# An FFT filter ahead of a Gelu layer: table loads and table builds of the first batch put in another order

## Chip, cores, metric

The kernel runs on one core of one Trainium2 chip. The metric is the device time of one execution in microseconds (us). Each kernel is run several times; a single run scatters by some tenths of a us, and some runs by 1.5 to 3.8 us (told below), so parts of a us are read from traces, and times only confirm the sum.

## The reference

```python
X = np.fft.rfft(x, axis=1)                    # x: 8 batches, 3008 tokens, 256 channels
y = np.fft.irfft(X * (filt_r + 1j * filt_i)[None], n=3008, axis=1)
h = y.reshape(24064, 256) @ w_in              # 256 -> 2048
g = 0.5 * h * (1.0 + erf(h / sqrt(2)))        # exact Gelu
out = g @ w_out                               # 2048 -> 256
```

## The kernel before

The transform of 3008 = 47 x 64 points is done with matmuls in four stages. TensorE writes each result into a PSUM bank, and an *eviction* (`_evac`) copies it out, so that the bank can be used again; VectorE (DVE), ScalarE (ACT) and GpSimd (POOL) do the rest. Batch 0 has its own fast path (stages `c1` to `c4`, with transposes `c1t` and `c3t` between them), the *prelude*, in which nothing else can run. Then comes the *loop*: 47 tiles of 512 tokens, 16 slots each, with the two layers (`mm1` and Gelu, `mm2`) on TensorE in every slot; the transforms of the later batches (`s1` to `s4`) are put into chosen slots. The second layer starts at slot 16.

Sine and Gelu are functions of ACT. The trace has two table loads on ACT, one at the start (0.74 us) and one ahead of the first Gelu (29.66 us), each of 1.28 us; the second is brought on by a dummy Gelu on one column.

```python
def table_2_sin(self, h):                     # half h of the second table
    self.nc.scalar.activation(out=self.T2[:, 12 * h:12 * h + 12, 1, :], in_=self.gen[:, h], func=AF.Sin, scale=2.0 * PI)

def table_3(self, q, eng):                    # 8 transposes, one eviction of 128x1024
    ps = self.bank("ps_t3", "n", BF16)
    for i in range(8):
        self.nc.tensor.transpose(ps[:, 128 * i:128 * i + 128], self.T2[:, 8 * q + i, 1:3]..., self.eye)
    self._evac(self.T3[:, 8 * q:8 * q + 8], ps..., eng)

def c2(self, p):                              # 4 matmuls of 256, then the product on VectorE
    ps = self.bank("ps_c2", "w")              # two buffers
    ...
    nc.vector.tensor_tensor(out=w, in0=ps, in1=f..., op=ALU.mult)   # f: filter rows, partly copied by GpSimd

# ---- prelude (cut) ----
m.dup_filters(nc.gpsimd, 4, 4); m.load_w_in(); m.dup_filters(nc.gpsimd, 8, 8)
for u in range(16):                           # first stage
    m.c1(u // 2, u % 2, act if u < 4 or u % 2 else False)
    ...
m.table_2_sin(1)
m.c1t(0, False); m.c1t(1, act)
for q in range(7):
    if q < 6:
        m.c2(2 * q)
        if q > 0 and q + 2 < 6: m.c1t(q + 2, act)
        m.c2(2 * q + 1)
    if q == 0: m.table_3(0, act); m.table_2_swap(1); ...; m.c1t(2, act)
    if 1 <= q < 3: m.table_3(q, act)
    if q >= 1:
        if q < 6: m.c3(2 * q - 2)
        else: m.table_4(); m.c3(10, 1); m.c3(11, 1)      # table_4 makes T4 and T4c
    if q == 4: nc.scalar.activation(out=warm, in_=m.p, func=AF.Gelu)
```

Products are counted from 0 in the code (`c2(4)` makes the fifth). The pool "n" of `c1t`, `c3` and the tables has four PSUM banks.

Of the kernel before, what the change touches and what calls it, by code (L numbers as in the profile page):

```python
# [9 lines left out]
AF = mybir.ActivationFunctionType  # L10
ALU = mybir.AluOpType
FP32 = mybir.dt.float32
BF16 = mybir.dt.bfloat16
# [4 lines left out]
NA, NB = 47, 64  # L18
K1 = 24
# [9 lines left out]
class _Mix:  # L29
# [187 lines left out]
        ts(out=self.wtc, in0=self.p, scalar1=4.0, scalar2=1.0, op0=ALU.is_ge, op1=ALU.add)  # L217


    def table_4(self):  # L220
        nc = self.nc
        ps = self.bank("ps_t4", "n")
        rows = ((self.T4, self.T1p, self.wt), (self.T4c, self.T1q, self.wtc))
        o = [ps[0:96, 128 * i:128 * i + 2 * NA] for i in range(2)]
        for i, (t4, t1, wt) in enumerate(rows):
            nc.tensor.matmul(o[i], lhsT=t1.rearrange("p a b c -> p (a b c)"),
                             rhs=self.eye[0:2 * NA, 0:2 * NA], start=True, stop=True)
        for i, (t4, t1, wt) in enumerate(rows):
            self._evac(t4.rearrange("p n h -> p h n"), o[i].rearrange("p (h n) -> p h n", h=2), "act", wt[0:96])

    def table_3(self, q, eng):
        ps = self.bank("ps_t3", "n", BF16)
# [277 lines left out]
@with_exitstack  # L510
def kernel(
    ctx: ExitStack,
    tc: tile.TileContext,
    x: bass.AP,
    filt_r: bass.AP,
    filt_i: bass.AP,
    moe_w_in: bass.AP,
    moe_w_out: bass.AP,
    out: bass.AP,
):  # L520
    m = _Mix(ctx, tc, x, filt_r, filt_i, moe_w_in, moe_w_out, out)
    nc, B, S = tc.nc, m.B, m.S
    NT = B * S // TCH
    ctx.enter_context(tc.manual_schedule())

    g = m.small
    wide = ctx.enter_context(ExitStack())
    m.psum(wide, w=(2, 2), n=(4, 1))
    act = "act"
    m.p = m.iota(g, "p", [128, 1], [[0, 1]], cm=1)  # L530
    m.load_x(0, 0, 1, (0,))
    m.pi = m.iota(g, "pi", [128, 1], [[0, 1]], cm=1, dt=I32)
    m.load_x(0, 0, 1, (1,))
    m.ones = g.tile([128, 512], BF16, name="ones")
    nc.vector.memset(m.ones, 1.0)
    m.warm_up(10)
    m.table_1(g)
    m.weights_4(g)
    m.T1c = g.tile([2 * NA, 96], BF16, name="T1c")
    nc.vector.tensor_copy(out=m.T1c.rearrange("p (k h r) -> p k h r", h=2, r=2),  # L540
                          in_=m.T1.rearrange("p (h r k) -> p k h r", h=2, r=2))
    m.kk = m.iota(g, "kk", [128, K1 // 2], [[1, K1 // 2]])
    m.jj = g.tile([128, NB], FP32, name="jj")
    for sgn, lo in ((1, 0), (-1, 32)):
        nc.gpsimd.iota(m.jj[:, lo:lo + 32], pattern=[[sgn * NA, 32]], base=min(0, sgn * NA),
                       channel_multiplier=0, allow_small_or_imprecise_dtypes=True)
    cols = m.iota(g, "cols", [128, 128], [[1, 128]])
    m.load_x(0, 1, 4)
    m.gen = m.py.tile([128, 3, K1 // 2, NB], FP32, tag="y", name="gen")
    m.table_2(g)  # L550
    m.table_2_angle(0)
    m.unit_matrices(g, cols)
    m.table_2_angle(1)
    for k, n in ((0, 4), (4, 4), (8, 8), (16, 8)):
        m.load_filters(k, n)
    m.dup_filters(nc.gpsimd, 4, 4)
    m.load_w_in()
    m.dup_filters(nc.gpsimd, 8, 8)


    warm = g.tile([128, 1], FP32, name="warm")
    for u in range(16):
        m.c1(u // 2, u % 2, act if u < 4 or u % 2 else False)
        if u == 3:
            m.warm_up(3)
            m.table_2_sin(0)
        if u == 7:
            m.table_2_swap(0)
            m.table_2_minus()
            m.warm_up(3)  # L570
        if u == 11:
            m.warm_up(2)
    m.table_2_sin(1)
    m.warm_up(2)
    m.c1t(0, False)
    m.c1t(1, act)
    m.dup_filters(nc.vector, 0, 4)
    for q in range(7):
        if q < 6:
            m.c2(2 * q)  # L580
            if q > 0 and q + 2 < 6:
                m.c1t(q + 2, act)
            m.c2(2 * q + 1)
        if q == 0:
            m.table_3(0, act)
            m.table_2_swap(1)
            m.dup_filters(nc.gpsimd, 16, 8)
            m.T1p = g.tile([2 * NA, 2, K1, 2], BF16, name="T1p")
            nc.gpsimd.tensor_copy(out=m.T1p, in_=m.T1.rearrange("p (h r k) -> p h k r", h=2, r=2))
            m.T1q = g.tile([2 * NA, K1, 2, 2], BF16, name="T1q")  # L590
            nc.gpsimd.tensor_copy(out=m.T1q, in_=m.T1.rearrange("p (h r k) -> p k r h", h=2, r=2))
            m.table_1_tiles(g)
            m.load_x(1)
            m.load_w_out(0)
            m.load_w_out(8)
            m.c1t(2, act)
        if 1 <= q < 3:
            m.table_3(q, act)
        if q >= 1:
            if q < 6:  # L600
                m.c3(2 * q - 2)
            else:
                m.table_4()
                m.c3(10, 1)
                m.c3(11, 1)
        if q == 4:

            nc.scalar.activation(out=warm, in_=m.p, func=AF.Gelu)
    wide.close()
    wide = ctx.enter_context(ExitStack())  # L610
    m.psum(wide, v=(5, 1), t=(3, 1))
    for u in range(10):
        if u < 8:
            m.c3t(u)
        if u >= 2:
            m.c4(u - 2, (act, False if u > 7 else act))
    wide.close()
    m.psum(ctx, h=(3, 1), o=(2, 1), f=(3, 1))


    at = {}

    def put(slot, f, *a):
        at.setdefault(slot, []).append((f, a))

    def first(b):
        return (b * S // TCH) * 16

    for b in range(1, B):
        hi = first(b)  # L630
        if b == 1:
            s1, n1, r1, s2, n2, r2, s4, n4 = 0, 4, 15, 25, 2.8, 61, 68, 0.72
        else:
            s1, n1, r1, s2, n2, r2, s4, n4 = hi - 94, 3.5, hi - 80, hi - 69, 3.5, hi - 24, hi - 17, 1
        for u in range(16):
            put(s4 + int(u * n4), m.s4, b, u // 2, u % 2)
        for c in range(4):
            put(s1 + int(c * n1), m.s1, b, c)
            put(r1, m.r1, b, c)
            put(r2, m.r2, b, c)  # L640
        for p in range(12):
            put(s2 + int(n2 * p), m.s2, b, p)
            put(s2 + int(n2 * p) + 4, m.s3, b, p)
        if b + 1 < B:
            for i in range(8):
                put(s2 + int(n2 * (i + 2)), m.load_next, b, i + 2, i // 2, i % 2)

    for s in range((NT + 1) * 16):
        t, jc = s // 16, s % 16
        for f, a in at.pop(s, ()):  # L650
            f(*a)
        if t >= 1:
            m.mm2(t - 1, jc)
        if t < NT:
            m.mm1(t, jc)
    assert not at
# [30 lines left out]
```

## Time and profile before

| what | before |
|---|---|
| median of four runs (lowest, highest) | 774.23 us (774.01, 775.79) |
| span of the profiled run; granted clock of TensorE, as a share of full speed | 772.4 us; 1.000 |
| first `c1t` matmul (end of the first stage) | 14.22 us |
| VectorE's products | 16.40 to 31.84 us |
| transposes `c3t` start | 33.55 us |
| y of batch 0 complete | 40.96 us |
| first second-layer matmul (slot 16) | 51.31 us |

The page's busy times say little here: TensorE is busy everywhere. The page of before:

```profile
PE 757.2 (98%) x5965; PEld 528.4 (68%) x6066; DVE 397.8 (52%) x722; ACT 567.0 (73%) x980; POOL 64.8 (8%) x161
```

What matters is that the profile names no wait of TensorE after slot 16, and that the 51 us ahead of it are a relay between four engines. The moments of the table are read from the engines' timelines (start of the row, or start plus length).

### The profile page before, as it was taken

To read this page: it belongs to the slowest core of one execution; us is meant where nothing else is said; L and a number is where in the kernel's file an instruction comes from. 1 tells how busy PE (TensorE), PEld (TensorE's weight loads), DVE (VectorE), ACT (ScalarE), POOL (GpSimd) and SP (SyncE) were. 2 spreads that over 40 slices of the span, in tenths; PEclk is the share of its full clock that TensorE was granted. 3 is DMA by queue.
4 is the path that set the end of the run, shared out by engine and by line. 5 is a ranking of instruction groups with operands and counts; after the bars stand their busy time and mean duration, and the time that the engine had idled before them with its cause. 6 is when DMAs were issued, how large, how long until landed. Compare 5 with 4: busy or idle time off the path is not lost.

```text
span 772.4 us, 14959 instructions
## 1 busy us (share of the span) xinstructions
PE 757.2 (98%) x5965; PEld 528.4 (68%) x6066; DVE 397.8 (52%) x722; ACT 567.0 (73%) x980; POOL 64.8 (8%) x161
## 2 busy tenths in 40 slices
PE   7899999999999999999999999999999999999998
PEld 4857775676776766677777776666776676766666
DVE  8866755464555645456463664637646366411011
ACT  6879955897568975699656996579865798666663
POOL 8801100020000200011000110001100000000000
PEclk9999999999999999999999999999999999999999
DMA  9895645456153661636516364254543422410111
GB/s 144 138 179 133 146 119 129 128 121 155 56 139 108 138 152 46 191 81 123 143 52 182 85 133 123 78 155 97 122 137 80 139 83 69 123 42 28 42 42 55
DMA packets 87398, 85.66 MB, mean 111 GB/s; under 512 B 6752, under 2 KB 77536, under 8 KB 87328
## 3 DMA queue, kind: packets, MB, share of 16 engines
q1 hardware_dynamic: 78816, 68.70, 31.2%
q0 software_dynamic: 8512, 16.00, 14.1%
q8 instruction: 47, 0.77, 0.4%
q14 instruction: 23, 0.19, 0.1%
HBM read 54.00 MB, written 46.66 MB: 130 GB/s over the span
## 4 chain that ended last, share of the span: by engine, by line
PE 96%; ACT 1%; DVE 1%; issue 1%; POOL 0%; DVEq 0%; POOLq 0%
PE ps_o L492 43%; PE ps_h L465 39%; PE ps_s L324 3%; PE ps_s L349 3%; PE ps_s L299 2%; PE ps_s L276 2%; PE ps_c L409 1%; PE ps_c L387 0%; PE ps_c3t L428 0%; ACT T L249 0%; PE ps_c L442 0%; ACT vt_sb L249 0%; PE ps_e L482 0%; PE ps_c1t L375 0%; ACT at_sb L249 0%
## 5 line engine op out<-in xcount | busy, mean ns | idle before, releaser
L468 ACT ACTIVATE g_sb<-ps_h 128x512 bf16<-128x512 f32 x752 | 437.9, 597 | 183.0 <-PE ps_h L465 154.6
L492 PE MATMUL ps_o<-w_out_sb,g_sb 128*128 128x256 bf16 x2992 | 447.5, 273 | 2.1
L465 PE MATMUL ps_h<-y_sb,w_in_sb 128*128 128x512 bf16 (+3 forms) x1500 | 424.2, 365 | 0.2 <-issue 0.2
L492 PEld LDWEIGHTS <-g_sb 128*128 128x128 bf16 x2992 | 283.9, 98 | 134.4 <-issue 9.9
L465 PEld LDWEIGHTS <-w_in_sb 128*128 128x128 bf16 x1600 | 154.8, 98 | 23.2 <-issue 1.2
L498 DVE COPY ost<-ps_o 128x512 f32<-128x512 f32 x93 | 63.9, 687 | 143.8 <-PE ps_o L492 143.7
L307 DVE TENSOR_TENSOR p<-ps_s,F 128x512 bf16<-128x512 f32 x84 | 58.1, 692 | 105.2 <-ACT p L306 89.1
L253 DVE TENSOR_SCALAR y_sb<-ps_s 128x376 bf16<-128x376 f32 x112 | 61.0, 548 | 80.5 <-PE ps_s L349 80.5
L251 DVE CAST a_sb<-ps_s 128x512 bf16<-128x512 f32 x112 | 69.5, 684 | 27.4 <-PE ps_s L276 27.1
L251 DVE CAST v_sb<-ps_s 128x512 bf16<-128x512 f32 x84 | 57.4, 685 | 2.9 <-PE ps_s L324 2.8
L305 ACT ACTIVATE p<-ps_s 64x512 bf16<-64x512 f32 x84 | 49.8, 593 | 2.0
L306 ACT CAST p<-ps_s 64x512 bf16<-64x512 f32 x84 | 48.5, 577 | 1.0
L349 PEld LDWEIGHTS <-d_sb 96*128 96x128 bf16 x448 | 30.8, 97 | 25.2
L101 POOL COPY gate<-p 1x1 bf16<-1x1 bf16 x48 | 8.5, 176 | 470.5 <-DVE p L309 470.5
L349 PE MATMUL ps_s<-T,d_sb 96*128 96x94 bf16 x448 | 36.3, 204 | 1.1
L309 DVE TENSOR_TENSOR p<-p 128x512 bf16<-128x512 bf16 x84 | 35.7, 425 | 2.9
L308 DVE TENSOR_TENSOR p<-p,F 128x512 bf16<-128x512 bf16 x84 | 34.9, 415 | 0.0
L324 PE MATMUL ps_s<-p,T 128*128 128x256 bf16 x168 | 32.1, 273 | 2.1
L82 POOL DMA_DIRECT2D x_sb<-in_x_dram x64 | 32.5, 510 | 13.3 <-issue 12.9
L299 PE MATMUL ps_s<-b_sb,T 128*128 128x256 bf16 x168 | 32.1, 273 | 0.0
L324 PEld LDWEIGHTS <-T 128*128 128x128 bf16 x168 | 16.4, 98 | 19.8 <-DVE p L309 0.4
L299 PEld LDWEIGHTS <-T 128*128 128x128 bf16 x168 | 16.4, 98 | 13.4
(103 smaller groups left out, 189.1 us busy)
## 6 DMA issues: line engine op xcount, KB each, us to landing
out_dram<-ost SPq DMA_DIRECT2D x93, 256.0 KB, 2.3
x_sb<-in_x_dram POOLq DMA_DIRECT2D x64, 188.0 KB, 3.6
R<-a_sb SPq DMA_DIRECT2D x112, 96.0 KB, 2.1
b_sb<-R SPq DMA_DIRECT2D x28, 384.0 KB, 4.3
R<-v_sb SPq DMA_DIRECT2D x42, 256.0 KB, 3.3
d_sb<-R SPq DMA_DIRECT2D x56, 192.0 KB, 4.6
w_in_sb<-in_moe_w_in_dram POOLq DMA_DIRECT2D x2, 512.0 KB, 7.5
w_out_sb<-in_moe_w_out_dram POOLq DMA_DIRECT2D x2, 512.0 KB, 12.6
```

Source lines behind the costliest of these rows:

```text
L251: self.nc.vector.tensor_copy(out=out, in_=in_)
L253: self.nc.vector.tensor_scalar(out=out, in0=in_, scalar1=scale, scalar2=None, op0=ALU.mult)
L299: nc.tensor.matmul(ps[:, 256 * i:256 * i + 256], lhsT=self.T2[:, k, 1:3].rearrange("p a b -> p (a b)"), rhs=self.st[b, "b", k // 6][:, k % ...
L305: nc.scalar.activation(out=p2[0:64], in_=ps[64:128], func=AF.Copy, scale=-1.0)
L306: nc.scalar.copy(out=p2[64:128], in_=ps[0:64])
L307: nc.vector.tensor_tensor(out=p1, in0=ps, in1=f(0), op=ALU.mult)
L324: nc.tensor.matmul(ps[:, 256 * i:256 * i + 256], lhsT=self.T3[:, k].rearrange("p a b -> p (a b)"), rhs=w[:, 256 * i:256 * i + 256], start= ...
L349: nc.tensor.matmul(ps[:, 94 * i:94 * i + 94], lhsT=d[:, (grp % 2) * 4 + i, 128 * half:128 * half + 128], rhs=t4, start=True, stop=True)
L465: nc.tensor.matmul(ps[:, o:o + n], lhsT=self.w_in_sb[:, dc, jc * 128:jc * 128 + 128], rhs=self.ring[:, dc, off:off + n], start=(dc == 0), ...
L468: nc.scalar.activation(out=self.st["g", t][:, jc, :], in_=ps, func=AF.Gelu)
L492: nc.tensor.matmul(ps[:, tile_i % 2, :], lhsT=g[:, jc, tile_i * 128:tile_i * 128 + 128], rhs=self.w_out_sb[:, jc, :], start=(jc == 0), sto ...
L498: nc.vector.tensor_copy(out=ost, in_=ps)
```

## The change

Its intent: put ACT's work where ACT idles, so that the Gelu load and the late tables leave the end of the prelude. Cut to its core:

```diff
+            m.table_2_sin(1)                       # at u == 7, inside the first stage
-    m.table_2_sin(1)
+    nc.scalar.activation(out=warm, in_=m.p, func=AF.Gelu)
...
+    nc.scalar.copy(out=m.T1q, in_=m.T1...)         # was a GpSimd copy
...
-        if 1 <= q < 3:
-            m.table_3(q, act)
+        if q == 2:
+            m.table_3(1, act)
+        if q == 4:
+            m.table_3(2, act)
+            m.table_4(m.T4c, m.T1q, m.wtc)
...
-                m.table_4()                        # ahead of c3(10) and c3(11)
-            nc.scalar.activation(out=warm, in_=m.p, func=AF.Gelu)   # end of q == 4
...
-            s1, n1, r1, s2, n2, r2, s4, n4 = 0, 4, 15, 25, 2.8, 61, 68, 0.72
+            s1, n1, r1, s2, n2, r2, s4, n4 = 1, 4, 16, 26, 2.8, 61, 68, 0.72
...
+    put(20, m.table_4, m.T4, m.T1p, m.wt, "f")     # T4 in the loop, slot 20
```

GpSimd's later copies and loads also stand ahead of the q loop in the program, in the same order on GpSimd.

More of the change, by code (lines that the diff above doesn't have):

```diff
@@ L217, in weights_4, with table_4 @@
         ts(out=self.wtc, in0=self.p, scalar1=4.0, scalar2=1.0, op0=ALU.is_ge, op1=ALU.add)
-    def table_4(self):
-        nc = self.nc
-        ps = self.bank("ps_t4", "n")
-        rows = ((self.T4, self.T1p, self.wt), (self.T4c, self.T1q, self.wtc))
-        o = [ps[0:96, 128 * i:128 * i + 2 * NA] for i in range(2)]
-        for i, (t4, t1, wt) in enumerate(rows):
-            nc.tensor.matmul(o[i], lhsT=t1.rearrange("p a b c -> p (a b c)"),
-                             rhs=self.eye[0:2 * NA, 0:2 * NA], start=True, stop=True)
-        for i, (t4, t1, wt) in enumerate(rows):
-            self._evac(t4.rearrange("p n h -> p h n"), o[i].rearrange("p (h n) -> p h n", h=2), "act", wt[0:96])
+    def table_4(self, t4, t1, wt, tag="n"):
+        ps = self.bank("ps_t4", tag)
+        self.nc.tensor.matmul(ps[0:96, 0:2 * NA], lhsT=t1.rearrange("p a b c -> p (a b c)"),
+                              rhs=self.eye[0:2 * NA, 0:2 * NA], start=True, stop=True)
+        self._evac(t4.rearrange("p n h -> p h n"), ps[0:96, 0:2 * NA].rearrange("p (h n) -> p h n", h=2), "act",
+                   wt[0:96])
     def table_3(self, q, eng):
@@ L577 @@
     m.dup_filters(nc.vector, 0, 4)
-    for q in range(7):
+    m.T1q = g.tile([2 * NA, K1, 2, 2], BF16, name="T1q")
+    nc.scalar.copy(out=m.T1q, in_=m.T1.rearrange("p (h r k) -> p k r h", h=2, r=2))
+    m.dup_filters(nc.gpsimd, 16, 8)
+    m.T1p = g.tile([2 * NA, 2, K1, 2], BF16, name="T1p")
+    nc.gpsimd.tensor_copy(out=m.T1p, in_=m.T1.rearrange("p (h r k) -> p h k r", h=2, r=2))
+    m.table_1_tiles(g)
+    m.load_x(1)
+    m.load_w_out(0)
+    m.load_w_out(8)
+    m.c2(0)
+    m.c2(1)
+    m.table_3(0, act)
+    m.table_2_swap(1)
+    m.c1t(2, act)
+    for q in range(1, 7):
         if q < 6:
             m.c2(2 * q)
-            if q > 0 and q + 2 < 6:
+            if q + 2 < 6:
                 m.c1t(q + 2, act)
             m.c2(2 * q + 1)
-        if q == 0:
-            m.table_3(0, act)
-            m.table_2_swap(1)
-            m.dup_filters(nc.gpsimd, 16, 8)
-            m.T1p = g.tile([2 * NA, 2, K1, 2], BF16, name="T1p")
-            nc.gpsimd.tensor_copy(out=m.T1p, in_=m.T1.rearrange("p (h r k) -> p h k r", h=2, r=2))
-            m.T1q = g.tile([2 * NA, K1, 2, 2], BF16, name="T1q")
-            nc.gpsimd.tensor_copy(out=m.T1q, in_=m.T1.rearrange("p (h r k) -> p k r h", h=2, r=2))
-            m.table_1_tiles(g)
-            m.load_x(1)
-            m.load_w_out(0)
-            m.load_w_out(8)
-            m.c1t(2, act)
-        if 1 <= q < 3:
-            m.table_3(q, act)
-        if q >= 1:
-            if q < 6:
-                m.c3(2 * q - 2)
-            else:
-                m.table_4()
-                m.c3(10, 1)
-                m.c3(11, 1)
-        if q == 4:
-            nc.scalar.activation(out=warm, in_=m.p, func=AF.Gelu)
+        if q == 2:
+            m.table_3(1, act)
+        if q == 4:
+            m.table_3(2, act)
+            m.table_4(m.T4c, m.T1q, m.wtc)
+        if q < 6:
+            m.c3(2 * q - 2)
+        else:
+            m.c3(10, 1)
+            m.c3(11, 1)
     wide.close()
```

## The prediction

> **What bounds the kernel now.** I read the core's clock first (1.000 throughout, span 772.4 us), then the chain of waits, then the timelines of the single engines. The change touches the first 44 us (the transform of batch 0) and some 30 slots of the loop that follows, so the first question is whether anything after that can move. The chain between 50 and 130 us answers it:
>
> ```profile
> by line: PE ps_o L492 44.7%; PE ps_h L465 40.9%; PE ps_s L324 3.9%; PE ps_s L349 3.8%; PE ps_s L299 3.3%; PE ps_s L276 2.8%; issue 0.8%
> ```
>
> Every entry is TensorE work; a list of TensorE's waits from 51 us to the end is empty. The loop is one unbroken stream of matmuls, of fixed length. The kernel's time is therefore the moment at which TensorE starts slot 16 (the chain has its first second-layer matmuls at 51.47 us) plus a constant, and a gain or loss in the prelude passes through one to one. Nothing here can be worth 2% (15.5 us) unless it breaks that stream.
>
> In the prelude the chain names these steps:
>
> ```profile
> 11.45 0.50 ACT at_sb L249
> 12.00 0.33 PE ps_c L365 x4
> 12.33 0.43 PE ps_warm L243 x2
> 12.77 0.34 PE ps_c L365 x4
> 13.14 1.03 DVE at_sb L251 x2
> ...
> 19.70 0.93 ACT b_sb L249
> 20.66 0.83 PE ps_c L409 x12
> ...
> 28.55 1.09 ACT vt_sb L249 x2
> 29.66 1.28 ACT L608
> ```
>
> Start, length, engine and tile. Three things are to be seen. At 11.45 an ACT eviction holds a PSUM bank for TensorE. At 19.70 the third-stage matmuls (L409) wait for an ACT eviction that frees a bank. At 29.66 the table load for Gelu (L608) sits on the chain itself. The ACT timeline shows what follows it:
>
> ```profile
> 29.66 1.28 ACT L608 ACT_TABLE_LOAD   x1
> 30.95 0.20 ACT L608 ACTIVATE warm<-p 128x1 f32<-128x1 f32 x1
> 31.06 1.06 ACT L249 ACTIVATE vt_sb<-ps_c 128x512 bf16<-128x512 f32 x2
> 32.02 0.36 ACT L249 ACTIVATE T<-ps_t,wt 96x94 bf16<-96x94 f32 x1
> 32.24 0.36 ACT L249 ACTIVATE T4c<-ps_t,wtc 96x94 bf16<-96x94 f32 x1
> 32.46 0.92 ACT L249 ACTIVATE vt_sb<-ps_c 128x256 bf16<-128x256 f32 x3
> ```
>
> The transposes after this start at 33.55. But ACT is not alone there. VectorE's products with the filters are nearly without a pause:
>
> ```profile
> 16.40 4.82 DVE L392 TENSOR_TENSOR p<-ps_c,F 128x1024 bf16<-128x1024 f32 x4
> 22.03 2.51 DVE L392 TENSOR_TENSOR p<-ps_c,F 128x1024 bf16<-128x1024 f32 x2 [0.81 <-PE ps_c L387]
> 24.84 5.81 DVE L392 TENSOR_TENSOR p<-ps_c,F 128x1024 bf16<-128x1024 f32 x5 [0.30 <-POOL F L96]
> 30.57 1.28 DVE L396 TENSOR_TENSOR p<-ps_c,F 128x512 bf16<-128x512 f32 x2
> ```
>
> From 16.40 to 31.85 they idle 1.1 us in two holes. The last product cannot end much before 31, whatever ACT does. The releaser of the second hole is, I think, TensorE and not GpSimd: the second-stage group at 24.15 ends at 24.75, and in the first hole the product also follows its group's end (21.93) by 0.1 us.
>
> **What the Trainium skill says.** "ScalarE: Activation LUTs", section What ACT_TABLE_LOAD costs: about 1283 ns for the load and some 1380 ns of drain, 2.66 us per switch. The trace has the 1.28 us, but not the drain as lost time: the eviction before ends at 29.64, the load starts at 29.66, and the eviction after it starts at 31.06, so a switch with its dummy activation costs 1.42 us here. I use that. The same page, section Table sets: the hidden batching unit, says that cheap functions such as copy are in every set. That is what makes an early Gelu load sound: after 29.66 the trace shows copies only, then Gelu at 42.27, with no further load. "TensorE: Matmul & The Clock Gate", section Wait — 56ns, not 53.3ns?: warm matmuls start every N/2.4 GHz + 2.5 ns. The trace agrees: 8 transposes of 128 columns take 0.45 us on the chain (56 ns each), 4 matmuls of 256 take 0.44 us. So moved TensorE work can simply be added.
>
> **The change, part by part.**
>
> *Second sine table at the eighth unit.* 0.84 us of ACT moves from 14.07 to just after the first swap's evictions, which end at 10.94; its angles are ready at 10.92. ACT was idle 0.52 us until 11.45 there, so the next eviction starts at about 11.79, 0.34 us late. TensorE waited for that eviction (12.00), and VectorE's last two evictions of the first stage follow TensorE (12.77 + 0.34, then 13.14). If the banks are handed out as before, the first stage ends 0.3 us later. Cost: 0 to 0.3 us.
>
> *Gelu table early.* It starts after the last first-stage eviction on ACT (14.2 to 14.5) and takes 1.42 us, to 15.6 to 15.9. The eviction of the second transposed block stood at 15.32; it slips by 0.2 to 0.5 us, but its reader, the third product's matmul, came only at 17.71. T1q's copy on ACT (about 0.3 us, from 0.36 for the 96x94 evictions) fits before 17.14, where ACT had idled 0.79 us for the first third-stage table. So both are hidden, and 1.42 us leave the end of the chain.
>
> *Third-stage tables in another order.* Each is 0.45 us of TensorE (8 transposes) and about 0.91 us of ACT (start to start, 21.35 to 22.25). Table 1 moves out of q = 1 and table 2 out of q = 2, into q = 2 and q = 4. The first third-stage group then gets its banks from the swap's evictions (ending at about 20.0 with the delay) instead of waiting until 20.66. Then the fifth second-stage group starts near 20.95 instead of 21.33, when ACT's b eviction is out. The product it feeds could start at 21.6, but needs the copied filter rows for its frequencies, which GpSimd finishes at about 21.92 (the first of eight copies that start at 20.86). So the hole of 0.81 us shrinks only to the same 21.95 that it ends at now (22.03): gain 0.1 us, and a start that is late by 0.3 us costs nothing here. The hole of 0.30 us at 24.53 closes, since q = 2 has enough lead. In exchange q = 4 now carries 0.45 us of transposes and the 0.05 us of the fourth table before its third-stage group of 1.0 us. Added up from 26.8 (end of product 7): 0.44 second-stage, 0.45, 0.05 to 0.1, 1.0, then the matmuls of product 10, ready 0.53 us after they start: 29.36, while VectorE is free at 29.13. A hole of about 0.2 us opens. VectorE's end: 31.85 - 0.1 - 0.3 + 0.2 = 31.65, give or take 0.2.
>
> *The tail.* From VectorE's end to the transposes it is 1.70 us now (31.85 to 33.55), because ACT has two evictions of 512, T4, T4c and three of 256 queued behind the table load. Freed of load and tables, ACT reaches the last group's evictions when TensorE has made them: 0.3 us of matmuls, 0.4 us of the eviction of 128x256 (0.42 on DVE), 0.1 of latencies, and 0.2 to 0.3 us for ACT's queue, so 1.0 to 1.1 us. Gain 0.65.
>
> *Fourth table deferred.* Off ACT's path in the tail (counted). In the loop it adds one matmul, 0.05 us, to a TensorE without gaps; its eviction of 0.25 us lies in ACT's pauses of 0.27 us a slot.
>
> *First-stage units of batch 1 one slot later.* Same TensorE work in another order. The first matmuls of the layer no longer stand behind eight first-stage ones with 0.16 us of issue at 41.65; ACT's first Gelu comes 0.6 us earlier. Gain 0.1 to 0.2 us, not more, as TensorE's sum over tile 0 is unchanged.
>
> **Sum.** 0.2 (VectorE's end) + 0.65 (tail) + 0.15 (order of the first slots) - 0.05 (T4 in the loop) = 0.95 us. 774.19 - 0.95 = 773.24; I say 773.2.
>
> **Rivals.**
> *ACT's chain was the whole bound:* the removed load (1.42 us), the two tables (0.45 us) and the bank wait at 20.66 come off in full, with the early sine hidden. For it: the chain of waits runs through ACT at 29.66 to 32.6. Against it: VectorE's 15.2 us of products from 16.40 must still run, and the last one waits for GpSimd's copies until 28.76 at least. It would make 772.2.
> *VectorE is the bound and its end moves late:* the 0.3 us of the early sine and the crowded q = 4 (0.2 to 0.4 us) eat the tail's gain. For it: the products are 99% packed after 24.84. It would make 773.8 to 774.2.
> *The first slots of the loop:* the shifted units could collide with the second layer's start (slot 16), or the reloaded rows arrive after slot 26. The stores' queue ends at 53.4 and the reads are issued from 55.22, 3.7 us ahead of their first use at 58.9; shifting unit, read and use by one slot each keeps the distance, and the interval between unit and use grows by half a slot. A miss would cost up to 1 us: 774.5.
>
> **Range and chances.** The sum's terms are uncertain by about 0.3 us each, and half of them lean against each other, so 8 in 10 within 772.3 and 774.1. Both ends are inside 0.3% of before, far from 2% on either side: same 0.99.
>
> **What would show it.** Right: the table load near 14.3 and the next ACT eviction at about 15.8; no TensorE wait of half a microsecond near 20.1 to 20.7; VectorE's products 4 to 9 without a hole and the last one ending at 31.4 to 31.9; the transposes of vt starting at 32.5 to 32.9; the second layer's first matmuls at about 50.5. Wrong: the first-stage end moving from 14.17 by more than 0.4 us; a hole over 0.5 us in the products in q = 4; any TensorE wait after slot 16; or the transposes starting a full 1.4 us earlier, which would mean that VectorE's end was not the limit.

## The result

The changed kernel took 773.63 us in the median of four runs (773.49 to 773.98), the kernel before 774.23; ratio 0.9989, interval 0.9971 to 1.0006. In a second set it was 773.70 against 774.54, ratio 0.9979 (0.9962 to 0.9996). A ratio is the mean time of one kernel's fast runs over that of the other's of the same rounds, so it is not quite the ratio of the medians. The gain in the medians is thus 0.6 to 0.8 us of 774, though the interval of the first set takes in a gain of nothing; the prediction said 773.2 with 772.3 to 774.1.

The first profile of the changed kernel fell on its slowest run, in which the rows of x landed late (first stage over at 14.53 us). The second profile (run a1 below) had the first stage over at 14.28 us, as good as before's 14.22, and is used here. Its ACT timeline, where the load is now:

```profile
14.26 1.28 ACT L571 ACT_TABLE_LOAD   x1
15.66 1.00 ACT L245 ACTIVATE b_sb<-ps_c1t 128x1024 bf16<-128x1024 bf16 x1
16.56 0.35 ACT L577 COPY T1q<-T 94x96 bf16<-94x96 bf16 x1
17.20 1.02 ACT L245 ACTIVATE T<-ps_t 128x1024 bf16<-128x1024 bf16 x1 [0.29 <-PE ps_t L230]
```

ACT still idles 0.29 us ahead of the first third-stage table, so load and copy are hidden. VectorE's products in the same run:

```profile
16.46 4.82 DVE L388 TENSOR_TENSOR p<-ps_c,F 128x1024 bf16<-128x1024 f32 x4
22.01 6.88 DVE L388 TENSOR_TENSOR p<-ps_c,F 128x1024 bf16<-128x1024 f32 x6 [0.73 <-POOL F L96]
29.19 1.23 DVE L388 TENSOR_TENSOR p<-ps_c,F 128x1024 bf16<-128x1024 f32 x1 [0.30 <-POOL F L96]
30.33 1.28 DVE L392 TENSOR_TENSOR p<-ps_c,F 128x512 bf16<-128x512 f32 x2
```

The hole ahead of the fifth product is nearly as long as before (0.73 for 0.81 us) and ends at the same time; the one ahead of the seventh has closed; a new one of 0.30 us stands ahead of the eleventh. The end is 31.61 us instead of 31.84. The end of ACT's queue:

```profile
28.68 0.35 ACT L245 ACTIVATE T4c<-ps_t,wtc 96x94 bf16<-96x94 f32 x1
28.90 1.07 ACT L245 ACTIVATE vt_sb<-ps_c 128x512 bf16<-128x512 f32 x2
30.25 1.91 ACT L245 ACTIVATE vt_sb<-ps_c 128x512 bf16<-128x512 f32 x5 [0.27 <-PE ps_c L405]
```

No load and no table stands in the last five evictions, and the transposes start at 32.58 us, 0.97 us after VectorE's end (1.71 before).

Here it should stop, but the gain of 0.97 us at the transposes is not the gain at the end. The start of the loop on TensorE, before:

```profile
41.02 0.63 PE L276 MATMUL ps_s<-x_sb,T1s 47*64 47x512 bf16 x8 [0.64 <-DVE y_sb L253]
41.80 1.71 PE L465 MATMUL ps_h<-y_sb,w_in_sb 128*128 128x512 bf16 x7 [0.16 <-issue]
...
51.31 0.60 PE L492 MATMUL ps_o<-w_out_sb,g_sb 128*128 128x256 bf16 x4
```

and changed (a1):

```profile
40.14 0.38 PE L461 MATMUL ps_h<-y_sb,w_in_sb 128*128 128x512 bf16 x1 [0.73 <-DVE y_sb L249]
40.66 0.63 PE L272 MATMUL ps_s<-x_sb,T1s 47*64 47x512 bf16 x8
...
50.51 0.60 PE L488 MATMUL ps_o<-w_out_sb,g_sb 128*128 128x256 bf16 x4
```

y is complete at 40.96 and 39.99 us. Before, the first matmul of the loop follows 0.06 us later and slot 16 10.35 us later; changed, 0.15 and 10.52 us. So 0.17 us of the gain are gone at slot 16.

The 0.16 us of "issue" in before's rows are no wait. Matmul records can be missing: the row has seven of eight first-layer matmuls. The same kernel in run c4, where all 32 ahead of slot 16 are recorded (30 in the profile above), has none:

```profile
42.92 0.63 PE L276 MATMUL ps_s<-x_sb,T1s 47*64 47x512 bf16 x8 [0.64 <-DVE y_sb L253]
43.48 1.72 PE L465 MATMUL ps_h<-y_sb,w_in_sb 128*128 128x512 bf16 x7
```

The first layer follows 0.56 us after the unit's start there, not 0.78: 0.22 us, the time of one matmul, were the missing record. The starts of the single matmuls also tell where the 0.17 us go: 0.09 us to the later start after y (0.15 for 0.06 us), and 0.08 us to one change more from the first layer to a first-stage unit ahead of slot 16 (four for three; such a change takes 0.31 us from start to start, two first-layer matmuls 0.22).

Then VectorE at the last product of batch 1; before, and changed (a1):

```profile
91.99 0.69 DVE L307 TENSOR_TENSOR p<-ps_s,F 128x512 bf16<-128x512 f32 x1 [0.23 <-issue]
...
93.39 0.68 DVE L498 COPY ost<-ps_o 128x512 f32<-128x512 f32 x1
```

```profile
91.80 0.68 DVE L494 COPY ost<-ps_o 128x512 f32<-128x512 f32 x1
92.39 0.68 DVE L303 TENSOR_TENSOR p<-ps_s,F 128x512 bf16<-128x512 f32 x1
```

Moved to slot 56, the last product stands behind the output copy of slot 55; its third-stage matmuls wait, and TensorE with them. From the first to the sixth output copy it is 39.98 us before and 40.12 us changed. All later output copies keep their distance to before to 0.01 us in the first profile of the changed kernel; in a1 another 0.05 us go ahead of the seventh, where the weights of a fourth-stage matmul of batch 1 wait 0.4 us for the read of d_sb. In the five other profiles with batch 1's products shifted, 0 to 0.12 us go there; in the eight with the old product slots, none.

**The chain of waits misleads in the changed kernel.** In the page of its first profile the chain begins:

```profile
PE 94%; DMA 3%; POOL 2%; issue 0%; DVE 0%; POOLq 0%
```

A chain that runs through the x loads of batch 1 and GpSimd's copies would mean that the prelude is bound by them. The wait that leads there is the one of the first layer's first matmul. TensorE's waits from 39 to 42 us in run b1 and in run b3:

```profile
PE ps_h L461 <- DMA x_sb<-in_x_dram: 0.7, 1, 0.7
```

```profile
PE ps_h L461 <- DVE y_sb L249: 0.7, 1, 0.7
```

It is the same wait, put down to a transfer in one run and to VectorE in the other. In all seven profiles with this order of the first slots, the matmul starts 0.14 to 0.15 us after VectorE's last y eviction. It is VectorE's; a transfer that lands near the same time took the name.

### The profile page after: what moved, and what is told of

It reads as the page before. It is cut to its first block, busy times and chain, and to the rows that moved or that the text cites. A ratio compares the mean times of both kernels' runs of the same rounds, so it can differ in the third digit from the quotient of the medians.

```text
span 772.2 us, 15059 instructions
## 1 busy us (share of the span) xinstructions
PE 763.2 (99%) x6066; PEld 528.7 (68%) x6066; DVE 397.3 (51%) x722; ACT 567.4 (73%) x981; POOL 64.9 (8%) x160
## 4 chain that ended last, share of the span: by engine, by line
PE 94%; DMA 3%; POOL 2%; issue 0%; DVE 0%; POOLq 0%
PE ps_o L488 43%; PE ps_h L461 42%; PE ps_s L345 2%; PE ps_s L320 2%; PE ps_s L295 2%; PE ps_s L272 2%; DMA x_sb<-in_x_dram 2%; POOL F L96 1%; POOL x_sb L82 1%; DMA F<-in_filt_i_dram 1%; POOL F L91 0%; PE ps_e L478 0%; POOL T1s L258 0%; DVE ost L501 0%; POOL T1p L580 0%
## 5 line engine op out<-in xcount | busy, mean ns | idle before, releaser
L461 PE MATMUL ps_h<-y_sb,w_in_sb 128*128 128x512 bf16 (+3 forms) x1600 | 445.8, 366 | 0.7 <-DMA x_sb<-in_x_dram 0.7
```

Of the source, the lines that this page charges most:

```text
L461: nc.tensor.matmul(ps[:, o:o + n], lhsT=self.w_in_sb[:, dc, jc * 128:jc * 128 + 128], rhs=self.ring[:, dc, off:off + n], start=(dc == 0), ...
```

## The experiments

Twelve runs. Two things disturb them and are left out of the comparison by reading stretches. First, x lands late by chance, which moves the end of the first stage. Second, if TensorE stands long enough for that, its clock can fall: in a second profile of the kernel before (c4) it waited 1.88 us, the clock was 0.50 from 10 to 12 us, the first stage ended at 16.05 us, and the run took 776.26 us (in a2 a wait of 1.80 us left it at 1.00). Such runs carry the state "fast" (c4, a single run, "unknown"), but a mean clock of 0.993 to 0.998; where I give a median "at full clock", it is over the runs with 1.000. Even that lets one through: b2's profiled run has 1.000 recorded, but its second group of 16 first-stage matmuls took 1.44 us, as c1's did at a recorded 0.53 to 0.50, against 0.84 us in before. The three sets of experiments ran on three chips, and before's own median at full clock was 774.47 us beside a1 to a4, 774.61 beside b1 to b4 and 774.24 beside c1 to c4, so medians compare within a set only. The stretches, all in us:

| run | first stage ends | VectorE, fifth product to end | from there to transposes | y complete to slot 16 | output copies 1 to 6 | median at full clock |
|---|---|---|---|---|---|---|
| before | 14.22 | 9.81 | 1.71 | 10.35 | 39.98 | 774.24 to 774.61 in three sets |
| before again (c4) | 16.05 | 9.82 | 1.70 | 10.34 | 39.98 | - |
| changed | 14.53 | 9.60 | 0.96 | 10.52 | 40.13 | 773.63 |
| changed again (a1) | 14.28 | 9.60 | 0.97 | 10.52 | 40.12 | 773.70 |
| a2, old slots | 14.51 | 9.60 | 0.97 | 10.34 | 39.97 | 773.70 |
| a3, Gelu load alone | 15.92 | 9.82 | 1.54 | 10.33 | 39.97 | 774.15 |
| a4, sine late | 14.27 | 9.90 | 0.97 | 10.51 | 40.12 | 773.91 |
| b1, only s1 shifted | 14.17 | 9.60 | 0.97 | 10.52 | 39.98 | 773.58 |
| b3, T4 and T4c late | 14.48 | 9.56 | 1.19 | 10.51 | 40.12 | 773.94 |
| c2, Gelu load late | 14.04 | 9.60 | 1.79 | 10.52 | 40.12 | 774.54 |

The other four runs (b2, b4, c1, c3) change when the fifth product starts, and their stretches are told with them below. The two profiles of before agree to 0.01 us in each stretch of the table although one lost 1.8 us in its first stage; so do the changed kernel's. That is what allows tenths to be told apart. It doesn't hold for every stretch: from the first product to the transposes, which some experiments below use, it is 16.12, 16.13, 16.27 and 16.32 us in a1, a2, the first profile and b1, whose preludes are the same, because GpSimd's copy for the fifth product starts 4.45 us after the first product in the first two and 4.65 us after it in the others. And from the sixth output copy to the last, c4 is 0.23 us longer than before, with no edit.

**a1: the changed kernel again.** No edit.

> The changed kernel, unchanged, for a second profile. In the first one the rows of x landed late (the second group of first-stage matmuls started at 9.38 us instead of 8.62), and that run was the slowest of its four (773.98 us against 773.49 to 773.64). If the lateness was chance, the first stage ends at about 14.2 us here, the fifth product of VectorE starts at 21.9 to 22.0, and the ratio to before is about 0.9992 (gain 0.6 us). If the change itself delays the first stage (the early sine, cost up to 0.3 us), it ends near 14.5 again without a late x.

First stage 14.28 us, fifth product at 22.01, ratio 0.9979. The lateness of the first profile was chance. x was late here too at the second group (9.10 us), but the last group of the first stage started at 12.83 us, and the early sine is not seen at the first stage's end.

**a2: old slots for batch 1.**

```diff
- s1, n1, r1, s2, ... = 1, 4, 16, 26, ...
+ s1, n1, r1, s2, ... = 0, 4, 15, 25, ...
```

> Only the slots of batch 1 are put back (0, 15 and 25 instead of 1, 16 and 26). My theory: the shift gains nothing at slot 16 and puts the output copy of slot 55 ahead of the last product of batch 1 on VectorE, so that the last third-stage matmul waits; putting it back should gain 0.1 to 0.25 us over the changed kernel, and the offset of the output copies to before should stay the same from the first to the last one but for 0.04 us of the deferred table. The rival, that the shift is what makes the change a gain at all (the first layer no longer behind eight first-stage matmuls), expects it slower than the changed kernel by 0.1 to 0.2 us.

Both losses vanish: 10.34 us to slot 16, 39.97 us between the copies. The shift costs 0.31 us (0.17 + 0.14 to 0.15). The medians do not show it (773.70 for both), nor do they contradict it: 0.3 us is within their scatter. The rival's gain from the shift is in no stretch.

**a3: the kernel before with the Gelu load alone moved.**

```diff
     m.table_2_sin(1)
+    nc.scalar.activation(out=warm, in_=m.p, func=AF.Gelu)
...
-        if q == 4:
-            nc.scalar.activation(out=warm, in_=m.p, func=AF.Gelu)
```

> The kernel before with only the Gelu table moved to just after the second sine. My theory: the load leaves the tail, and the tail from VectorE's last product to the transposes falls from 1.70 us by 0.5 to 0.8 us, with VectorE's end nearly unmoved at 31.5 to 31.9; gain 0.5 to 0.8 us. The rival, that ACT's chain alone was the bound, expects the whole 1.42 us.

Both theories missed. The transposes come only 0.16 us earlier after the fifth product (11.36 against 11.52), and VectorE's stretch is unmoved. The ACT timeline of a3 tells why:

```profile
32.69 1.08 ACT L249 ACTIVATE vt_sb<-ps_c 128x512 bf16<-128x512 f32 x2 [1.24 <-PE ps_c L409]
33.66 0.36 ACT L249 ACTIVATE T<-ps_t,wt 96x94 bf16<-96x94 f32 x1
33.88 0.37 ACT L249 ACTIVATE T4c<-ps_t,wtc 96x94 bf16<-96x94 f32 x1
```

Where the load had stood, ACT now idles 1.24 us for TensorE's third-stage group. The load of 1.28 us had been hidden in that pause but for 0.16 us, although it stood on the chain of waits.

**a4: the changed kernel with the sine late.**

```diff
             m.warm_up(3)
-            m.table_2_sin(1)
...
+    m.table_2_sin(1)
     nc.scalar.activation(out=warm, in_=m.p, func=AF.Gelu)
```

> The changed kernel with the second sine back behind the first stage (and the Gelu load after it). If the early sine costs 0.3 us at the end of the first stage and this is hidden later behind GpSimd's copies, the time stays within 0.1 us of the changed kernel. If the early sine is needed to make room for the table load, the copy of T1q and the first third-stage table, this is slower by 0.3 us or more: the load then ends 0.8 us later, the b block is evicted at about 16.5 and the first third-stage table at about 17.9 instead of 17.45.

First stage 14.27 us, as in a1 with the sine early: the early sine costs nothing there. The load starts at 15.10 instead of 14.26, all of ACT's work behind it comes later, and the third-stage group waits for a bank again:

```profile
20.23 0.83 PE L405 MATMUL ps_c<-T,p 128*128 128x128 bf16 x12 [0.24 <-ACT T L245]
```

VectorE's stretch is 9.90 instead of 9.60 us, since a hole opens ahead of the seventh product. The transposes start at 32.80 instead of 32.58. So the early sine earns 0.22 us against a1. From the end of the first stage to the transposes it is 18.53 us here, 18.30 and 18.31 us in a1 and a2, but 18.46 and 18.49 us in the first profile and b1, where GpSimd's copy for the fifth product came later: 0.04 to 0.23 us, between the two expectations.

**b1: only the first-stage units of batch 1 shifted.**

```diff
- s1, n1, r1, s2, ... = 1, 4, 16, 26, ...
+ s1, n1, r1, s2, ... = 1, 4, 15, 25, ...
```

> The changed kernel with only the first-stage units of batch 1 one slot later; its reads and second-stage products stand at 15 and 25 again. My theory splits the cost of the shift in two: 0.17 us between the end of y and slot 16 (from the unit that no longer comes first) and 0.17 us at the last third-stage matmul of batch 1 (from the products that follow the output copy of slot 55). Here the first stays (10.5 us from the end of y to the first second-layer matmul, as in the changed kernel) and the second goes (the output copies stay 708.0 us apart from first to last, not 708.1). The rival, that both come from the first-stage units, expects both to stay.

10.52 us to slot 16 stays, the copies are 39.98 us apart. The two losses have two causes, as said.

**b2 and c3: GpSimd's filter copies ahead of its w_in load, old slots.** The same kernel twice.

```diff
     m.dup_filters(nc.gpsimd, 4, 4)
-    m.load_w_in()
     m.dup_filters(nc.gpsimd, 8, 8)
+    m.load_w_in()
```

> The changed kernel with the old slots, and with GpSimd's load of w_in behind the first four of the eight filter copies instead of ahead of them. If the hole of 0.73 us ahead of the fifth product is a wait for GpSimd's first copy, the copy ends 1.1 us earlier, the hole shrinks to 0.1 to 0.4 us (the second-stage matmuls, ready at about 21.3), and the last product ends 0.2 to 0.4 us earlier than in the changed kernel; the hole of 0.30 us ahead of the eleventh, which I put down to TensorE, stays or grows. If TensorE sets the pace in any case, the hole at the fifth only moves to later products and the end stays within 0.1 us.

> The copies-first kernel with the old slots a second time, because its profiled run had a late first stage (16.29 us). If its gains are real, the stretch from the first product to the transposes is again 15.9 us (16.1 with the copies as in the changed kernel), the loop keeps 10.35 us ahead of slot 16, and its fast runs lie at 772.8 to 773.4, 0.2 to 0.5 us below the changed kernel's.

In b2 the first stage ended at 16.29 us, so its hole (0.29 us) proves nothing. In c3 the first six products have no hole: the 0.73 us were a wait for GpSimd's copy. The hole of 0.30 us ahead of the eleventh stays. From the first product to the transposes it is 15.89 and 15.93 us, against 16.12 to 16.32 in the four profiles of the changed prelude: 0.2 to 0.4 us gained. But c3's profile shows a new wait in the loop, which takes the stretch to slot 16 to 11.36 us:

```profile
50.51 1.02 PE L461 MATMUL ps_h<-y_sb,w_in_sb 128*128 128x512 bf16 x4 [0.86 <-DVE a_sb L247]
```

VectorE had itself stood for 1.55 us there. The stores of a_sb took 4.6 us in the median from issue to landing up to 52 us, against 2.7 us in a2. That VectorE waited for a buffer held by such a store fits, but was not tested, and b2, the same kernel, has 2.9 us and no such wait (10.34 us to slot 16). Of the eleven runs four took 772.78 to 772.85 us and five 773.98 to 774.36; what parts them is not shown. The medians at full clock (773.34 and 773.98) are 1.27 and 0.26 us below before's in their sets, on either side of a1's 0.77, so no gain over the changed kernel is shown.

**b3: both fourth tables late.**

```diff
-            m.table_4(m.T4c, m.T1q, m.wtc)        # q == 4
...
+            m.table_4(m.T4, m.T1p, m.wt)          # ahead of c3(10, 1)
+            m.table_4(m.T4c, m.T1q, m.wtc)
-    put(20, m.table_4, m.T4, m.T1p, m.wt, "f")
```

> The changed kernel with both fourth tables back ahead of the last two third-stage groups. The run with the Gelu table alone moved took only 0.17 us off the tail, so I now think that the two tables hold the rest: 0.45 us of ACT ahead of the last evictions and the banks behind them. Then the tail from VectorE's last product to the transposes is 1.4 to 1.6 us here instead of 0.97, and the kernel is 0.4 to 0.6 us slower than the changed one. If the tables were hidden there, the tail stays below 1.1 us.

The tail is 1.19 us: the tables hold 0.22 us of it, less than I expected (0.18 from the fifth product to the transposes). a3 and b3 both have load early and tables late, but 1.54 and 1.19; what differs is the third-stage tables' order and the sine.

**b4: as b2, with the matmuls of product 10 ahead of the third-stage group of q = 4.**

```diff
-            m.c2(2 * q)
+            if q < 5: m.c2(2 * q)
...
             m.table_4(m.T4c, m.T1q, m.wtc)
+            m.c2(10)                              # q == 4, ahead of c3(6)
```

> As the copies-first kernel with the old slots, and with the second-stage matmuls of product 10 ahead of the third-stage group in q = 4. If the hole ahead of the eleventh product is a wait for TensorE and not for GpSimd, it closes; VectorE then ends 0.2 to 0.3 us earlier than in the copies-first kernel. Against before the whole should gain 1.1 to 1.5 us. If the matmuls that were put behind it make the tail late in their place, the gain is nil.

The hole ahead of the eleventh product is gone, so it was TensorE, and not GpSimd, whom the profile names. The gain is nil all the same: from the first product to the transposes 16.10 us (b2 15.89). VectorE's end did not move (14.99 us after its first product; b2 14.92, c3 14.96), since holes of 0.24 and 0.18 us stand ahead of the fifth and the ninth product instead, and the tail grew to 1.11 us. Median at full clock 773.75.

**c1: the old order of the third-stage tables.**

```diff
-        if q == 2: m.table_3(1, act)
-        if q == 4: m.table_3(2, act); ...
+        if 1 <= q < 3: m.table_3(q, act)
```

> The changed kernel with the third-stage tables 1 and 2 back at q = 1 and q = 2. I read the prelude from the start of VectorE's first product to the first transpose of vt, so that the chance landing of x does not count: 17.15 us before, 16.12 to 16.32 in four profiles of the changed order. If the order is what lets the Gelu load's removal pay, the third-stage group at 19.3 waits for an ACT eviction again, the fifth or seventh product waits for TensorE, and the stretch is 16.5 us or more (slower by 0.3 us or more). If GpSimd's first copy holds the fifth product in any case and q = 4 loses its 0.30 us hole, it is 16.2 or less.

Inconclusive. TensorE's clock was 0.50 from 10 to 14 us, and the first product started at 20.73 us, when GpSimd's copies no longer held anything. The stretch of 15.55 us is therefore not comparable. From the fifth product to VectorE's end it is 9.60 us and the tail 1.07, so 0 and 0.10 us worse than a1; but here TensorE had first stood 1.44 us for VectorE, so that proves little. Four of six runs had a lowered clock, and the two others took 774.19 and 775.36.

**c2: the changed kernel with the Gelu load late.**

```diff
-    nc.scalar.activation(out=warm, in_=m.p, func=AF.Gelu)
...
+        if q == 4:
+            nc.scalar.activation(out=warm, in_=m.p, func=AF.Gelu)
```

> The changed kernel with the Gelu load back at the end of q = 4, all else as changed. The run with the load alone moved gained only 0.05 us in that stretch (17.10 against 17.15). If the load was truly hidden before and the tables were the cost, the stretch stays at 16.1 to 16.4. If each of the two was covered by the other, so that only both together pay, it is 16.9 or more, because the load again stands ahead of the last two evictions of 512.

From the first product to the transposes 16.79 us, between the two expectations. The tail is 1.79 us instead of 0.97: with the rest of the change in place, the same load costs 0.82 us and not 0.16. ACT in c2:

```profile
29.64 1.28 ACT L606 ACT_TABLE_LOAD   x1
31.05 1.89 ACT L245 ACTIVATE vt_sb<-ps_c 128x512 bf16<-128x512 f32 x5
```

In a1 the corresponding evictions start at 30.25. TensorE is left with too little to do, and its clock pays (time, busy time of each engine, granted clock, share of DMA):

```profile
31.00:32.00 1.00, 0.32 (x4) 0.26 (x4) 0.27 (x1) 1.00 (x3) 1.00 (x3) 1.00 0.74 131
32.00:33.00 1.00, 0.45 (x6) 0.22 (x4) 0.41 (x1) 0.94 (x4) 1.00 (x3) 1.00 1.03 201
33.00:34.00 1.00, 0.94 (x10) 1.00 (x11) 0.01 (x1) 0.00 (x0) 1.00 (x2) 0.54 1.08 209
```

The transposes to y complete then took 8.91 us instead of 7.41.

**c4: the kernel before again.** No edit, one look.

> The kernel before, unchanged, for a second profile: the stretch from the first product to the transposes should be 17.1 to 17.2 us again, the stretch from the end of y to slot 16 10.35 us, and the one from the first to the sixth output copy 39.98 us, whatever the first stage does. If they scatter by more than 0.1 us, the splitting of the gain into parts is not to be trusted.

First product to transposes 17.09 us (before: 17.15), the other two stretches as expected to 0.01 us. Its span is 2.1 us longer (774.5 for 772.4): 1.83 us come from the first stage and 0.23 us from a pause ahead of a fourth-stage matmul at 287 us, which the first profile does not have.

## Why the prediction was right, and where it was not

The time lies in the range and the sign is right, but 773.2 was 0.4 us too low. The range ran from a gain of 0.1 us to one of 1.9 us, so landing in it says little; the terms say more. By its own terms, with the two profiles whose first stages ended alike (before and a1):

- *VectorE's end, 0.2 us:* measured 0.23 (31.84 to 31.61). The working held: the fifth product stayed bound to GpSimd's first copy (22.01; predicted 21.95), as c3 confirmed by removing that wait; the hole ahead of the seventh closed; one of 0.30 us (predicted 0.2) opened ahead of the eleventh, and b4 showed it to be TensorE's.
- *The tail, 0.65 us:* measured 0.74. The sum was right and its reason half right. I had taken load and tables as things to be freed of. Alone, the load is worth 0.16 us (a3), because ACT would have waited for TensorE anyway. With the rest of the change TensorE's group is there earlier and the load would be in the way: then it is worth 0.82 us (c2). The fourth tables are worth 0.22 us of the tail (b3). How much the third-stage tables' order adds by itself stays open, as c1 was disturbed.
- *The early sine, a cost of 0 to 0.3 us:* no cost (a1 against a4: 14.28 and 14.27), and a gain of 0.04 to 0.23 us later that I had not seen, since it makes the Gelu load early too.
- *The shifted slots, a gain of 0.1 to 0.2 us:* this step failed. I argued that the first layer would no longer stand behind eight first-stage matmuls with 0.16 us of issue. But those 0.16 us were a missing record and no wait (c4), so there was nothing to gain. TensorE does the same work in the other order, with one change more between the two kinds, and the first layer's start takes 0.15 us after y where the first-stage unit took 0.06. Result: 0.17 us lost (a2, b1). And one of the rivals named the wrong collision: I checked the transfers around slots 16 and 26, not VectorE's output copies, which stand at every eighth slot. The last product of batch 1 fell behind one: another 0.14 us lost (a2). The wait that this brings on TensorE after slot 16 (0.2 us in a1) was on my own list of signs of being wrong. Together -0.31 where I had put +0.15.
- *T4 in the loop, 0.05 us:* measured 0.05 (from slot 16 to the first output copy 6.71 us before, 6.76 with T4).

The sum with measured terms: 0.23 + 0.74 - 0.17 - 0.05 - 0.14 = 0.61 us, which is the distance of the sixth output copies (98.00 and 97.39); less the 0.05 ahead of the seventh it is 0.56 us. The last output copies of 128x512 in the two traces are 0.56 us apart (765.94 and 765.38). Two figures of the prediction do not add up, without bearing on its sum: the rows of VectorE's products come to 14.4 us, not 15.2, and the matmuls of product 10 to 29.27 to 29.32 us, not 29.36. The gain expected by the rival "ACT's chain was the whole bound" (2 us) did not come; it was partly VectorE, as I had said, and partly that the load was hidden.

## What to carry to other kernels

A block on the chain of waits is worth its length only if nothing else would have held its engine: look at what its successor waits for once it is gone, and expect two changes that cover each other to pay only together. When work moves by one slot in a saturated loop, check it against everything periodic on the engine that serves it, not only against its own inputs. And with effects of tenths of a us under chance of whole ones, compare stretches between events in traces, after showing that two traces of one kernel agree in them.

## What the Trainium skill lacked or had wrong

- "ScalarE: Activation LUTs", What ACT_TABLE_LOAD costs: it gives 2.66 us for every switch, drain included. Here the load took 1.28 us and a switch with its dummy activation 1.40 to 1.42 us from eviction to eviction (29.64 to 31.06 before); no 1.38 us of drain were lost beside it. What a switch costs the kernel was 0.16 us or 0.82 us, by what ACT would have waited for.
- "TensorE: Matmul & The Clock Gate", What's actually happening: it gives an idle window of some 3.4 us as what halves the clock. In c2 TensorE was not idle for such a time, but busy 0.71, 0.32 and 0.45 us in the three us from 30 on, with waits of 0.93 and 0.51 us; the clock of 33 to 34 us was 0.54. In c4 it waited 1.88 us, was 0.62 us busy of the 2 us from 8 on, and the clock of 10 to 12 us was 0.50. Runs of the kernel before with a mean clock of 0.993 to 0.998 took 775.8 to 777.9 us, those with 1.000 774.1 to 775.3.
- No page says that a releaser in the profile can be another event that came near it: the same 0.73 us wait for y was named an x transfer in some profiles and VectorE in others, and the chain of waits followed the transfer back to the start of the kernel.
- No page says that a trace can lack a matmul record and so show an idle time that wasn't: 30 of 32 first-layer matmuls ahead of slot 16 are recorded in one profile of before, with "0.16 us of issue", and 32 in the other, without it.
